# A gated recurrence with a gated convolution: one exponential for two chunks, products in place, other rings and a new order

## The chip, the core and the metric

The kernel runs on one core of a Trainium2 chip. The metric is the device time of one execution in microseconds (us). The core has five instruction queues that run side by side and meet only at semaphores: PE (matmuls and transposes; PEld is its weight load), DVE, ACT (activation functions by table), POOL and SP (which here only issues transfers). Each queue works strictly in the order in which its instructions were written.

## What is computed

Inputs are x, r_gate and i_gate, each 4 x 6336 x 256 in float32, and small weights. With c = 8:

```python
log_a = c * sig_r * np.log(a_base)          # a_base = sigmoid(a_param), clipped
a_t = np.exp(log_a)
norm = np.sqrt(np.maximum(1.0 - a_t * a_t, 1e-06))
x_gated = norm * sig_i * x
h = a_t[:, t] * h + x_gated[:, t]           # for each t in a sequence
```

Then the states h pass a causal convolution of 5 taps for each of the 256 channels; its sigmoid is the gate, and the output is (gate * (h @ w_val)) @ w_out, again 4 x 6336 x 256 in float32.

## The kernel before

The 25,344 rows of the four sequences are one line of time. It is cut into 50 windows of 512 rows (the last has 256), and the windows into 27 chunks: windows 0 and 1 are a chunk each, then come 23 chunks of two windows, then window 48 and window 49. Channels are handled as two halves of 128.

A window passes these steps. `lr`, `li`, `lx` load r, i and x (512 KB each; issued on SP, `load`). `th` makes the tanh of half of r and i in one ACT instruction of 2048 columns (L292); a sigmoid is half of that plus one. The gated input u is (tanh + 1) * x: either POOL does it in two instructions (`pp`, L300, and `up`, L312) or DVE in two of 512 columns (`uv`, L317). For a chunk, `tr` transposes the tanh of r on PE so that channels lie on the partitions (L326), and `ex` makes the decay a of it, one ACT exponential for each half, read from a PSUM bank and written to the ring `aring` (L333), with scale and bias taken for each partition from `khf`. `sq`, `sv` or `sa` square the decay on POOL (L344), DVE (L348) or ACT (L352) into `ering`. `rt` takes the square root of 1 - a*a for a batch of chunks (mostly three, six windows) on ACT (L363); it needs another function table, so each of the eleven batches has a table load ahead of it and one behind it (L495). `nt` transposes the norm back (L376), `xg` multiplies it with u on DVE (L383), `xt` transposes the product (L394), and `sc` runs the recurrence over a chunk and a half as one scan on DVE (L415), into `yring`. Where that ring starts again, a copy of its last four columns goes ahead (L411, on ACT, eight times). `cv` is the convolution as matmuls with diagonal weights (L427), `tg` its tanh (L434), `vl` the value product (L442), `gv` gate times value on DVE (L447), `ou` the output matmuls in two parts (L458), `cd` or `ca` copies each part out of PSUM on DVE or ACT (L466, L468), and `st` stores the window.

Every ring is a tile with a fixed number of slots: `riring` and `xring` four windows, `tring` three, `uring` ten, `xgring`, `tgring` and `gvring` two, `oring` four. A step that fills a slot waits until the step that last read it is done. PSUM has eight banks, and the words of the order name which a step uses.

The order of all instructions is one written list, `ORDER`; there is no planner at work when the kernel is built. A word such as `tr.8@6,7` is a step, its window or chunk, and its banks. The words of one engine, taken in the order of the list, are that engine's queue; `lr`, `li`, `lx` and `st` are SP's.

Of the kernel before, what the change touches and what calls it, by code (L numbers as in the profile page):

```python
# [8 lines left out]
P = 128  # L9
# [14 lines left out]
NU = 10  # L24
# [3 lines left out]
NXG = 2  # L28
NTG = 2
NGV = 2  # L30
NOSB = 4

ORDER = """
s_ident s_small s_kt s_diag li.0 lr.0 th.0 li.1 lr.1 th.1 pp.1 lr.2 li.2 tr.0@0,1 tr.1@2,3 ex.0.1 sq.0.1 ex.0.0 sq.0.0
s_wl.2 lx.2 li.3 lx.0 li.4 th.2 ex.1.0 sv.1.0 ex.1.1 rt.0 sv.1.1 rt.1 lx.1 uv.0 lr.3 nt.0@3 xg.0 lr.4 nt.1@2 xt.0@1,0
th.3 up.1 xg.1 xt.1@3,2 uv.2 th.4 li.5 pp.4 tr.2@4,5 lr.5 th.5 ex.2.1 ex.2.0 lx.3 tr.3@6,7 ex.3.0 sc.0.1 uv.3 lx.4
li.7 up.4 s_wl.0 lr.7 ex.3.1 th.7 lr.6 sa.3.1 li.6 th.6 tr.4@6,7 sq.2.0 lx.5 s_wl.3 sv.2.1 sv.3.0 rt.2 uv.5 sc.1.1
sc.0.0 cv.0@0,1 lx.6 sc.1.0 nt.2@3 s_wl.1 s_wcast pp.6 lx.7 lx.8 li.8 uv.7 li.10 li.9 lr.8 lr.9 ex.4.1 lr.10 li.11
nt.3@2 ex.4.0 nt.5@4 xg.2 xg.3 xt.2@3,2 th.8 sc.2.0 xg.5 tg.0 vl.0@6,7 gv.0 up.6 pp.8 th.9 tr.5@0,1 nt.4@3 xg.4 th.10
cv.1@4,5 sq.4.1 up.8 ex.5.1 lr.11 th.11 tr.6@3,1 ou.0.0@6 ou.0.1@7 lx.10 ex.5.0 tg.1 lx.9 ex.6.1 ex.6.0 uv.10 uv.9  # L40
sc.2.1 cd.0.0 li.13 li.12 lr.12 lr.13 xt.3@4,5 vl.1@0,1 cv.2@2,3 gv.1 sc.3.0 li.14 lr.14 sc.3.1 lx.14 lx.13 li.15
th.12 li.16 lx.12 th.13 lx.11 lr.17 lr.15 lr.16 tg.2 cv.3@0,1 tg.3 tr.7@6,4 ex.7.1 vl.2@2,3 ex.7.0 li.17 ou.1.0@0
pp.11 sq.5.0 sq.6.1 sq.6.0 sq.5.1 sq.4.0 pp.12 rt.3 cv.4@4,5 gv.2 tg.4 ou.2.0@6 cd.2.0 pp.13 ou.1.1@1 vl.3@2,3 gv.3
up.12 cd.1.1 cd.1.0 cd.0.1 st.1 up.11 sq.7.1 th.14 ou.3.1@2 ou.3.0@3 cd.3.0 cd.3.1 th.15 st.0 st.3 ou.2.1@1 cv.5@6,7
tg.5 cd.2.1 st.2 up.13 lx.17 nt.7@2 xg.7 nt.6@1 xg.6 pp.14 up.14 pp.15 vl.4@2,3 gv.4 nt.8@1 xt.4@4,5 xg.8 th.16 lx.16
pp.16 vl.5@2,3 li.18 lx.15 li.19 lr.19 nt.9@1 tr.8@6,7 ex.8.0 sc.4.0 sq.8.0 th.17 sc.4.1 lr.18 ou.4.1@0 cd.4.1
ou.4.0@4 lr.21 xg.9 lr.20 li.20 gv.5 cv.7@5,6 ex.8.1 tg.7 cd.4.0 st.4 xt.5@0,1 ou.5.0@2 sc.5.1 cd.5.0 sc.5.0 pp.17
up.16 sq.8.1 cv.6@3,4 sa.7.0 ou.5.1@7 tg.6 cd.5.1 tr.9@5,6 ex.9.0 nt.10@1 xg.10 up.15 vl.6@2,3 ex.9.1 nt.11@4 st.5
vl.7@5,6 xg.11 cv.9@0,1 xt.6@7,4 th.19 li.23 gv.7 th.18 ou.7.0@5 gv.6 cv.8@2,3 li.21 sc.6.0 cd.7.0 tg.9 up.17 th.20
lx.18 lx.21 lx.20 li.22 tg.8 vl.9@0,1 ou.6.1@6 sc.6.1 ou.7.1@7 gv.9 cd.7.1 tr.10@2,3 cd.6.1 sq.9.0 ou.6.0@5 cd.6.0  # L50
vl.8@0,1 ou.9.0@7 lx.19 lr.22 gv.8 li.24 lr.24 ou.9.1@4 cd.9.1 cv.11@5,6 cd.9.0 st.7 st.9 st.6 ou.8.0@0 cd.8.0 sq.9.1
rt.4 nt.13@4 xg.13 nt.12@7 xg.12 pp.19 pp.20 up.20 pp.18 up.18 up.19 tg.11 ex.10.1 sq.10.1 vl.11@0,1 gv.11 th.21 pp.21
lr.25 nt.14@4 xt.7@7,6 up.21 cv.10@0,1 tg.10 ex.10.0 sq.10.0 th.22 ou.8.1@5 tr.11@0,1 nt.15@3 sc.7.1 sc.7.0 xg.15
vl.10@6,7 ou.11.1@3 ex.11.1 sq.11.1 ex.11.0 xg.14 xt.8@2,4 lr.23 gv.10 ou.10.0@6 lx.23 th.23 pp.23 up.23 lx.22
# [52 lines left out]
def kernel(  # L107
# [34 lines left out]
    def places(cap, lens):  # L142
        at, out = 0, []
        for n in lens:
            if at + n > cap:
                at = 0
            out.append(at)
            at += n
        return out

    a_at = places(NA, clen)
    e_at = places(NE, clen)

    segs, y_at, y_wrap = [], [], []
    at = 4
    for c in range(NCH):
# [370 lines left out]
```

## Time and profile before

| what | us |
|---|---|
| runs | 307.43, 307.86, 308.36 (median 307.86) |
| profiled execution, its time | 307.03 |
| profiled execution, its span | 305.2 |
| busy: ACT, DVE, PE, POOL | 284.7, 262.3, 241.6, 222.4 |
| moved by the transfers | 104.75 MB, mean 343 GB/s |

The span runs from the first to the last instruction; some 1.8 us lie around it. "Busy" counts instructions that compute. A row of the groups reads: line, engine, operation, output and inputs with their shapes, how many; then busy time of the group, mean duration of one in ns, and the idle time of the engine just before them with what ended it. A wait reads: who waited, for whom, us in total, how often, the longest.

### The profile page before, as it was taken

How to read it: one execution, taken by the hardware profiler on the slowest of the kernel's cores; microseconds unless marked ns; L12 is line 12 of the kernel's file. 1: busy time of each engine (PE TensorE's matmuls, PEld its weight loads, DVE VectorE, ACT ScalarE, POOL GpSimd, SP SyncE). 2: the span in 40 equal slices, each digit the busy share in tenths (PEclk: the TensorE clock that was granted, in tenths of full speed). 3: DMA queues.
4: the chain of work that ended last, by engine and by line, in shares of the span. 5: the costliest groups of instructions: out<-in, count | busy, mean ns of one | idle time of the engine just before them, and what ended most of it. 6: DMA issues, size and time to landing. Idle time of an engine off the chain costs nothing.

```text
span 305.2 us, 6266 instructions
## 1 busy us (share of the span) xinstructions
PE 241.6 (79%) x2463; PEld 165.8 (54%) x2463; DVE 262.3 (86%) x257; ACT 284.7 (93%) x234; POOL 222.4 (73%) x144
## 2 busy tenths in 40 slices
PE   0252386879698888978897996698998999999994
PEld 0241253546565656556664665466565675676663
DVE  2068895978999999899999999789999999999982
ACT  6899989999999998999999998989999999989664
POOL 1326636997999699999997899979996876626000
PEclk9998577999999999999999999979999999999999
DMA  7999999999999999999999799999999849633345
GB/s 266 390 409 404 389 407 362 414 407 402 349 414 341 412 350 415 372 410 412 379 410 407 294 384 387 396 338 413 400 406 383 269 183 307 246 140 141 137 164 216
DMA packets 29419, 104.75 MB, mean 343 GB/s; under 512 B 3271, under 2 KB 3790, under 8 KB 29390
## 3 DMA queue, kind: packets, MB, share of 16 engines
q1 hardware_dynamic: 29376, 104.35, 88.7%
q8 instruction: 19, 0.31, 0.4%
q14 instruction: 10, 0.08, 0.1%
q10 hardware_dynamic: 14, 0.01, 0.0%
HBM read 78.39 MB, written 25.95 MB: 342 GB/s over the span
## 4 chain that ended last, share of the span: by engine, by line
DMA 25%; PE 22%; ACT 17%; POOL 16%; issue 10%; DVE 7%; SPq 2%; ACTq 0%; POOLq 0%; DVEq 0%
DMA xring<-in_x_dram 15%; POOL uring L312 9%; ACT tring L292 8%; PE banks L427 8%; PE banks L458 6%; DMA riring<-in_r_gate_dram 5%; PE banks L442 5%; POOL ering L344 5%; ACT aring L333 4%; DMA out_dram<-oring 4%; POOL tring L300 3%; ACT tgring L434 3%; DVE uring L317 2%; PE banks L376 2%; DVE gvring L447 2%
## 5 line engine op out<-in xcount | busy, mean ns | idle before, releaser
L415 DVE TENSOR_TENSOR_SCAN yring<-aring,yring,banks 128x1024 bf16<-128x1024 f32 (+5 forms) x52 | 104.7, 2035 | 1.3 <-PE banks L394 1.1
L312 POOL TENSOR_TENSOR uring<-tring,xring 128x1024 bf16<-128x1024 bf16 (+1 forms) x43 | 91.1, 2132 | 17.5 <-DMA xring<-in_x_dram 16.5
L292 ACT ACTIVATE tring<-riring 128x2048 bf16<-128x2048 f32 (+1 forms) x50 | 93.6, 1901 | 5.8 <-DMA riring<-in_r_gate_dram 2.4
L344 POOL TENSOR_TENSOR ering<-aring 128x1024 f32<-128x1024 f32 (+2 forms) x47 | 84.9, 1826 | 13.2 <-ACT aring L333 13.1
L427 PE MATMUL banks<-yring,diag 64*64 64x512 bf16 (+7 forms) x1060 | 66.3, 376 | 7.6 <-ACT aring L333 2.0
L447 DVE SCALAR_TENSOR_TENSOR gvring<-tgring,banks 128x1024 bf16<-128x1024 bf16 (+1 forms) x50 | 59.2, 1201 | 7.8 <-PE banks L442 2.8
L300 POOL TENSOR_SCALAR tring<-tring 128x1024 bf16<-128x1024 bf16 (+1 forms) x43 | 44.3, 1039 | 24.7 <-ACT tring L292 24.6
L333 ACT ACTIVATE aring<-banks,khf 128x1024 f32<-128x1024 bf16 (+2 forms) x54 | 59.6, 1142 | 1.3 <-PE banks L326 1.2
L458 PE MATMUL banks<-wo,gvring 128*128 128x256 bf16 x396 | 54.9, 274 | 4.2 <-DVE gvring L447 2.9
L442 PE MATMUL banks<-yring,wv 128*128 128x512 bf16 (+4 forms) x212 | 50.2, 364 | 5.0 <-ACT tgring L434 2.5
L434 ACT ACTIVATE tgring<-banks 128x1024 bf16<-128x1024 f32 (+1 forms) x50 | 50.3, 1025 | 2.2 <-PE banks L427 1.7
L458 PEld LDWEIGHTS <-gvring 128*128 128x128 bf16 x396 | 41.6, 114 | 17.0 <-issue 7.2
L326 PE MATMUL banks<-ident_b,tring 128*128 128x128 bf16 x396 | 31.0, 232 | 24.9 <-ACT tring L292 19.1
L427 PEld LDWEIGHTS <-diag 64*64 64x64 bf16 x1060 | 31.3, 108 | 31.8 <-issue 17.8
L466 DVE COPY oring<-banks 128x512 f32<-128x512 f32 x68 | 44.1, 678 | 4.1 <-DMA out_dram<-oring 2.3
L363 ACT ACTIVATE ering<-ering 128x4096 bf16<-128x4096 f32 (+4 forms) x14 | 44.7, 3219 | 0.1
L376 PE MATMUL banks<-ident,ering 128*128 128x128 f32 x198 | 35.0, 307 | 10.7 <-ACT ering L363 8.0
L326 PEld LDWEIGHTS <-tring 128*128 128x128 bf16 x396 | 25.9, 104 | 31.6 <-ACT tring L292 23.3
L383 DVE TENSOR_TENSOR xgring<-banks,uring 128x1024 bf16<-128x1024 bf16 (+1 forms) x50 | 32.9, 675 | 9.2 <-POOL uring L312 4.2
L376 PEld LDWEIGHTS banks<-ident,ering 128*128 128x128 f32 x198 | 29.2, 207 | 18.6 <-ACT ering L363 10.3
L442 PEld LDWEIGHTS <-wv 128*128 128x128 bf16 x212 | 19.7, 98 | 23.3 <-issue 10.2
L394 PE MATMUL banks<-ident,xgring 128*128 128x128 f32 x198 | 27.8, 279 | 3.1 <-DVE xgring L383 2.0
(35 smaller groups left out, 110.6 us busy)
## 6 DMA issues: line engine op xcount, KB each, us to landing
riring<-in_i_gate_dram SPq DMA_DIRECT2D x49, 512.0 KB, 7.5
riring<-in_r_gate_dram SPq DMA_DIRECT2D x49, 512.0 KB, 7.8
xring<-in_x_dram SPq DMA_DIRECT2D x49, 512.0 KB, 7.9
out_dram<-oring SPq DMA_DIRECT2D x49, 512.0 KB, 6.3
oring<-in_moe_w_val_dram SPq DMA_DIRECT2D x1, 256.0 KB, 5.9
riring<-in_r_gate_dram SPq DMA_DIRECT2D x1, 256.0 KB, 6.3
riring<-in_i_gate_dram SPq DMA_DIRECT2D x1, 256.0 KB, 6.3
xring<-in_x_dram SPq DMA_DIRECT2D x1, 256.0 KB, 3.6
```

The costliest lines, as they stand in the source:

```text
L292: nc.scalar.activation(out=tring[:, w % NTRI, :, 0:J, :], in_=riring[:, w % NRI, :, 0:J, :], func=ACT.Tanh, scale=0.5)
L312: nc.gpsimd.tensor_tensor(out=u, in0=t1, in1=xt, op=ALU.mult)
L326: nc.tensor.transpose(out=bank[:, o:o + P], in_=tring[:, w % NTRI, 0, j, h * P:(h + 1) * P], identity=ident_b[:])
L333: nc.scalar.activation(out=aring[:, h, a_at[c]:a_at[c] + clen[c]].rearrange("c (w p j) -> c w p j", w=nw, p=P), in_=bank[:, 0:clen[c]].rea ...
L344: nc.gpsimd.tensor_tensor(out=e, in0=a, in1=a, op=ALU.mult)
L376: nc.tensor.transpose(out=bank[:, (q * H + h) * P:(q * H + h + 1) * P], in_=ering[:, o + h * clen[c] // 2 + q:o + h * clen[c] // 2 + wins[ ...
L415: nc.vector.tensor_tensor_scan(out=yring[:, h, col:col + o1 - o0], data0=aring[:, h, a_at[c] + o0:a_at[c] + o1], data1=xT[:, o0:o1], initi ...
L427: nc.tensor.matmul(out=gp[oh * 64:oh * 64 + 64, h, a:b], lhsT=diag[half * 64:half * 64 + 64, h, k, :], rhs=yring[half * 64:half * 64 + 64, ...
L434: nc.scalar.activation(out=tgring[:, w % NTG, :, 0:wins[w]], in_=live.pop(("gp", w))[:, :, 0:wins[w]], func=ACT.Tanh, scale=0.5)
L442: nc.tensor.matmul(out=val[:, m, a:b], lhsT=wv[:, hk, m * P:(m + 1) * P], rhs=yring[:, hk, col:col + b - a], start=(hk == 0), stop=(hk == ...
L447: nc.vector.scalar_tensor_tensor(out=gvring[:, w % NGV, :, 0:wins[w]], in0=tgring[:, w % NTG, :, 0:wins[w]], scalar=1.0, in1=live.pop(("va ...
L458: nc.tensor.matmul(out=ops[:, e * D:(e + 1) * D], lhsT=gv[:, hk, j:wins[w]:J], rhs=wo[:, hk, :], start=(hk == 0), stop=(hk == H - 1))
```

## The change

Groups of chunks are introduced. From chunk 2 to chunk 23 two neighbouring chunks form a group. The transposes of the tanh of r are now written for a group and one half at a time (`tr.c.h`), 16 of them into two neighbouring banks, and one exponential of 2048 columns reads both banks. Chunks 0, 1, 24, 25 and 26 stay alone. So 54 exponentials become 32.

To keep the tanh of r of four windows until then, a slot of `tring` gets three parts in place of two: i has the middle one, and r lies ahead of it or behind it, changing with each turn of the ring (`swapped`). The load puts r and i into `riring` in the matching order.

The product with the norm is written over u (`xgring` goes, `uring` gets 11 slots), and the gated value over the gate (`gvring` goes, `tgring` gets 3 slots). The 64-column identity of the set-up lies in an output slot. The eight copies at the wrap of `yring` move from ACT to DVE.

The list `ORDER` is another one throughout. By count, `ca` goes from 31 to 37 and `cd` from 68 to 62; `uv` from 7 to 10 windows, `pp` and `up` from 43 to 40; `sq` from 47 to 46, `sv` from 4 to 5, `sa` stays 3. Windows with `uv` were 0, 2, 3, 5, 7, 9, 10 and are 0, 2 to 7, 10, 12, 13. All other steps are as many as they were, and the same batches of square roots are taken.

```diff
-NU = 10
+NU = 11
-NXG = 2
-NTG = 2
-NGV = 2
+NTG = 3
+GROUPS = [[0], [1], [2, 3], [4, 5], [6, 7], [8, 9], [10, 11], [12, 13], [14, 15], [16, 17], [18, 19], [20, 21], [22, 23],
+    [24], [25], [26]]
...
-        tring = rings.tile([P, NTRI, 2, 4, D], BF16, name="tring")
-        xgring = rings.tile([P, NXG, 2, D, 2], BF16, name="xgring")
+        tring = rings.tile([P, NTRI, 3, 4, D], BF16, name="tring")
-        gvring = rings.tile([P, NGV, H, 512], BF16, name="gvring")
+        id64 = oring[:, 0, 0, 0:64]
...
+        def swapped(w):
+
+            return (w // NTRI) % 2
+
...
-                dst = riring[:, w % NRI, "ri".index(which), 0:J, :]
+                dst = riring[:, w % NRI, "ri".index(which) ^ swapped(w), 0:J, :]
...
-            nc.scalar.activation(out=tring[:, w % NTRI, :, 0:J, :], in_=riring[:, w % NRI, :, 0:J, :],
+            a = swapped(w)
+            nc.scalar.activation(out=tring[:, w % NTRI, a:a + 2, 0:J, :], in_=riring[:, w % NRI, :, 0:J, :],
...
+        def op_tr(c, h, *at):
+            ws = [w for k in sorted(group_of[c], key=lambda k: a_at[k]) for w in cwins[k]]
+            J = wins[ws[0]] // P
+            bank = banks[:, at[0]:at[-1] + 1].rearrange("c k n -> c (k n)").bitcast(BF16)
+            for g, w in enumerate(ws):
+                assert wins[w] == J * P
+                for j in range(J):
+                    o = (j * len(ws) + g) * P
+                    nc.tensor.transpose(out=bank[:, o:o + P],
+                                        in_=tring[:, w % NTRI, 2 * swapped(w), j, h * P:(h + 1) * P],
+                                        identity=ident_b[:])
+            live["rT", c, h] = bank
...
+            at = sorted(a_at[k] for k in group_of[c])
+            n = clen[c]
+            J = wins[cwins[c][0]] // P
+            src = bank[:, 0:n * len(at)].rearrange("c (j k q) -> c k q j", j=J, k=len(at))
...
+            nc.scalar.activation(out=dst, in_=src, func=ACT.Exp, scale=khf[:, h:h + 1], bias=khf[:, h:h + 1])
...
-            nc.vector.tensor_tensor(out=xgring[:, w % NXG, 0:nq].rearrange("p q d two -> p (q d two)"),
+            nc.vector.tensor_tensor(out=uring[:, w % NU, 0:nq].rearrange("p q d two -> p (q d two)"),
...
-                        nc.scalar.copy(out=yring[:, :, 0:4], in_=yring[:, :, e - 4:e])
+                        nc.vector.tensor_copy(out=yring[:, :, 0:4], in_=yring[:, :, e - 4:e])
...
-            nc.vector.scalar_tensor_tensor(out=gvring[:, w % NGV, :, 0:wins[w]],
+            nc.vector.scalar_tensor_tensor(out=tgring[:, w % NTG, :, 0:wins[w]],
```

## The prediction

> **What bounds the kernel now.** I read the busy shares first, then the groups with their shapes kept apart, then what ScalarE waited for, and last the stretches between the square-root batches (`rt.0` to `rt.10`). The busy shares:
>
> ```profile
> PE 241.6 (79%) x2463; PEld 165.8 (54%) x2463; DVE 262.3 (86%) x257; ACT 284.7 (93%) x234; POOL 222.4 (73%) x144
> ```
>
> ACT has 20.5 us free in the whole span, and DVE 42.9. The stretches below are cut where ACT loads the table for a batch of square roots (65.3, 97.0, 131.5, 156.7, 189.9, 225.4, 252.6 and 278.6 us, `rt.3` to `rt.10`); the columns are the start and end, the length, then busy time of PE, PEld, DVE, ACT and POOL, the granted clock, the DMA share and GB/s.
>
> ```profile
> 20.00:40.00 20.00, 8.09 (x78) 5.62 (x77) 16.08 (x15) 19.89 (x14) 12.85 (x10) 0.70 1.03 399
> 40.00:66.00 26.00, 19.91 (x189) 13.50 (x190) 20.79 (x18) 25.13 (x20) 18.08 (x12) 0.90 1.01 395
> 66.00:98.00 32.00, 27.12 (x267) 18.50 (x265) 29.83 (x29) 31.94 (x24) 30.05 (x19) 1.00 1.01 381
> ...
> 225.00:252.60 27.60, 25.85 (x289) 18.35 (x288) 27.00 (x27) 27.52 (x26) 21.38 (x14) 1.00 0.79 292
> 252.60:278.50 25.90, 25.04 (x256) 16.95 (x254) 25.05 (x21) 24.42 (x28) 14.24 (x12) 1.00 0.61 223
> 278.50:305.20 26.70, 22.44 (x232) 14.24 (x229) 19.32 (x18) 17.21 (x25) 2.53 (x2) 0.99 0.42 168
> ```
>
> There are two regimes. From 20 to 252.6 us ACT is full in every stretch (27.52 of 27.60). After 252.6 us it is PE: 25.04 of 25.90, then 22.44 of 26.70, of which the last 4 us are the final copy and store. The DMA share stands at about 1.0 up to 225 us, so the transfers are a close second, but ACT hardly waits for them:
>
> ```profile
> ACT oring L468 <- PE banks L458: 4.7, 7, 2.3
> ACT tring L292 <- DMA riring<-in_r_gate_dram: 2.4, 2, 1.5
> ACT tgring L434 <- PE banks L427: 1.7, 2, 1.2
> ...
> ACT tring L292 <- POOL ering L344: 1.2, 1, 1.2
> ...
> ACT tring L292 <- POOL uring L312: 0.7, 3, 0.3
> ```
>
> The rows that price the change (busy us of the group, mean ns of one):
>
> ```profile
> L292 ACT ACTIVATE tring<-riring 128x2048 bf16<-128x2048 f32 x49 | 92.6, 1918 | 5.6 <-DMA riring<-in_r_gate_dram 2.4 <-POOL ering L344 1.2 <-issue 0.8
> L333 ACT ACTIVATE aring<-banks,khf 128x1024 f32<-128x1024 bf16 x46 | 54.0, 1215 | 0.0
> ...
> L468 ACT COPY oring<-banks 128x512 f32<-128x512 f32 x31 | 17.5, 598 | 4.7 <-PE banks L458 4.7
> ...
> L333 ACT ACTIVATE aring<-banks,khf 128x512 f32<-128x512 bf16 x6 | 4.4, 774 | 1.2 <-PE banks L326 1.2
> ```
>
> **The change, ACT.** Twenty-two pairs of exponentials of 1024 columns become 22 of 2048 (11 groups, two halves). The exponential rows give (1215 - 774)/512 = 0.861 ns a column, so 2048 columns cost 1215 + 882 = 2097 ns, against 2 x 1215 = 2430: 333 ns saved. Neighbours overlap by 1215 - 54.0/46 = 41 ns, and one overlap goes with each merge: 292 ns, times 22 = 6.4 us off. No 2048-column exponential stands in the trace. At worst it costs the two it replaces (0 saved). At best it costs what the 2048-column tanh does, 1918 (22 x 471 ns = 10.4 saved). I keep 6.4, from the same instruction's own rows. Its source now steps over two PSUM banks, 1024 bytes between neighbours instead of 256; the slope above already holds for a stepped read, so I add nothing.
>
> ACT takes six output copies from DVE (37 against 31): 6 x 17.5/31 = +3.4. The eight tiny copies at the wrap of the y ring leave it (8 x 201 ns, -1.6). It squares three full chunks instead of two and a 256-column one (1069 - 437 ns, +0.6). Table loads stay at 22. Sum -4.0: ACT would be busy 280.7.
>
> What counts is where this falls. Ahead of `rt.9` (its table load at 252.57) stand all merges but also 15 output copies instead of 6 (+5.1), six of the tiny copies (-1.2) and the extra square (+1.1): -6.4 + 5.1 - 1.2 + 1.1 = **-1.4 us on the path**. The rest of the ACT relief lies behind 252.6 us, beside a full PE, and is worth nothing there.
>
> **DVE.** Minus six output copies (6 x 44.1/68 = -3.9). Ten windows instead of seven have their gated input made here: 6 more instructions of 512 columns, mean 11.9/14 = 0.85, +5.1 (717 ns at the least, 2449 at the most: +4.3 to +14.7). One more square of 1024 columns, +2.8 (twice the 692 ns of the 512 form to 2.91: +1.4 to +2.9). The eight wrap copies, nearest the 168 ns copy of 10 columns, +1.3 (from 62 ns, a memset: 0.5 to 1.6). Sum +5.3, DVE 267.6. About 7.9 of it lies before the batch at 65 us; later DVE gets lighter. Its cover is ACT's full queue; the rival below is that cover failing.
>
> **POOL.** Three windows leave: 3 x (1049 + 2155) = -9.6. Two full squares fewer and one more of 256 columns, -3.3. Sum -12.9, POOL 209.5. ACT waited 1.2 + 0.7 for POOL; I take half of that away, **-1.0**.
>
> **PE.** The same transposes and matmuls. By the written order the work behind `rt.9` is 42.0 us before and 41.9 after (counts of the steps, at 1.21 for a window's convolution, 0.86 for its value product, 0.44 for a half of its output, 0.47 and 0.43 for the two transposes, all from single pieces of the chain of waits), so the PE-bound end of 52.6 us stays: **0**. Each half's transposes now fill two banks and are read for 2.1 us instead of 1.2, so these banks come free later; other banks are named for the steps in between, and ACT's order keeps another ACT instruction between the last tanh of a group and its exponential in all groups but the first (chunks 2 and 3), where it waits for 4 transposes, 4 x 0.064 = 0.3.
>
> **Rings and products in place.** The product with the norm goes into the ring of gated inputs and the gated value into the ring of the gate. An in-place DVE instruction stands beside one that is not, on 2 columns (169 ns each), so the instruction costs 0; between a gain and a loss I see no row that excludes a few ns. What changes is when a slot is free: the gate's slot now waits for the output matmuls of three windows earlier, where it had waited for the product of two windows earlier; measured in ACT work of the written order these waits have a mean lead of 4.7 us against 5.8, and some leads of nothing in both. The r half of a tanh slot is kept for six windows instead of three, which is what a group of four windows needs. The identity of 64 columns moves into an output slot that the first output needs only after 57 us: 0.
>
> **SP.** The same 204 transfers in a new order. The first four loads are the same four, so the first tanh instructions do not move. Leads of loads ahead of their tanh, in ACT work, are 15.2 against 15.6 us on average, two landing times of 7.5; 0, with 1 us either way for a few that come close.
>
> **The sum.** -1.4 - 1.0 + 0 + 0 = -2.4. The profiled execution took 307.03 for its span of 305.2, so 304.6; the median of the runs shown, 307.86, lies 0.8 above that execution, and by it the change gives 305.4. I say 305.0.
>
> **The rivals.**
> DVE starts the kernel late. Up to 66 us DVE has 51 us from its first square at 14.95, is busy for 40.1 of them and idle for 11. The moved work of 7.9 fits if the idle time can be filled. But the tanh of a window overwrites the slot whose gated input of three windows before must have been read, and in the new order windows 2 to 7 have it read by DVE, so a late DVE stops ACT. If none of the idle can be used, 7.9 - 2.4 = +5.5; if the moved instructions all run at their dearest (14.7 + 2.9 = 17.6), 6.6 overrun the 11 and 6.6 - 2.4 = +4.2. Time 309 to 312.5. It decides from 2.4 us of lateness on. For it: of the idle time between 15 and 66 us, 4.2 are waits for POOL's products and 2.4 for loads of x, which DVE cannot fill at will. Against it: with three products fewer on POOL just there, the first of these should shrink.
> The Trainium skill, "SBUF — State Buffer", section "Who interferes with whom", has a rule that speaks for this rival: a VectorE instruction with two SBUF inputs contends with a GpSimd one that reads SBUF, and the later waits for the other's whole length. The trace agrees: while DVE's two full squares ran (27.02 to 32.63) a POOL square took 2.88 us against its mean of 1.93. By that rule alone all six would be dear, and the overrun of 6.6 the case to expect.
>
> The transfers bind. At 370 to 404 GB/s and a share of about 1.0 from 40 to 225 us, the loads may not come faster; then ACT's relief turns into waits for loads: 307.0 to 307.9. Against it: the stretch from 131 to 158 us ran at 404.
>
> The plan fits better everywhere: ACT's whole -4.0 and the 1.9 of POOL waits come off: 301.1 to 302.
>
> The merge does not pay: two banks read at the price of two exponentials, -2.4 + 6.4 = +4.0: 311.
>
> **How the numbers follow.** A measurement of this kernel can tell 0.3%, about 0.9 us, from no change. Forecast 0.42 (303 to 306.5), better plan 0.15, transfers 0.11, late DVE 0.28, no merge 0.04. Faster 0.57, same 0.11, slower 0.32. The range of 8 in 10 goes down to the forecast with the merge at its best price (4.0 more saved, 300.6), which takes in the better plan, and up to 312, all of the late DVE but its far end: 300.5 to 312.
>
> **What would show it.** The exponential row at 128x2048, x22, near 2.10 us; ACT busy near 281; the table load of `rt.9` near 250.2; PE full from there, for some 52 us. Against me: idle time of ACT's tanh put down to DVE before 70 us, instructions of the gated input on DVE near 2.4 us, or PE idle behind 252 us waiting for gates.

## The result and the profile after

The changed kernel takes 311.57 us (median of four runs, 310.63 to 312.62); the kernel before took 307.88 (307.43 to 308.36) beside it. The ratio is 1.012, with a 95% interval from 1.0084 to 1.0157: 3.7 us slower, where 2.9 us faster was forecast; the time lies within the forecast's range, on the other side of no change. The profiled execution of after took 311.38 us for a span of 309.6; before it was 307.03 for 305.2. Medians are of all executions; the ratios leave out those more than 1.5% above the fastest of their kernel, of which run a4 below had four in thirteen (312 to 320 us, its profiled one among them) and no other run more than one.

The busy shares of after:

```profile
PE 238.7 (77%) x2439; PEld 166.0 (54%) x2463; DVE 267.6 (86%) x266; ACT 283.1 (91%) x210; POOL 209.9 (68%) x137
```

ACT works 1.6 us less, DVE 5.3 more, POOL 12.5 less, in a span that is 4.4 us longer. So what was lost is idle time: ACT has 26.5 us of it, where it had 20.5. The groups of after by shape, first on ACT (the joined exponential, the output copies), then on DVE (gated input, wrap copy, squares); columns as before: busy us of the group, mean ns of one, idle time ahead of them:

```profile
L346 ACT ACTIVATE aring<-banks,khf 128x2048 f32<-128x2048 bf16 x22 | 44.7, 2060 | 2.1 <-DVE yring L425 1.1 <-PE banks L330 0.7
...
L478 ACT COPY oring<-banks 128x512 f32<-128x512 f32 x37 | 20.2, 595 | 3.2 <-DMA out_dram<-oring 2.0 <-PE banks L468 1.2
```

```profile
L319 DVE SCALAR_TENSOR_TENSOR uring<-tring,xring 128x512 bf16<-128x512 bf16 x20 | 15.4, 831 | 9.8 <-DMA xring<-in_x_dram 9.5 <-ACT tring L294 0.3
L421 DVE COPY yring<-yring 128x8 bf16<-128x8 bf16 x8 | 6.8, 854 | 0.0
L358 DVE TENSOR_TENSOR ering<-aring 128x1024 f32<-128x1024 f32 x3 | 5.3, 1758 | 0.0
```

All exponentials together went from 59.6 to 52.6 us, as the merge was meant to. One row stands out: a copy of 8 columns that takes 854 ns. The 9.5 us that the gated input on DVE waits for loads of x (2.4 before) came over from POOL with the work: POOL's own wait for x fell from 16.5 to 8.4 us, so that the two together wait 17.9 us where they waited 18.9. The stretches of after, the last three cut at the table loads of `rt.9` and `rt.10` (255.6 and 287.3 us):

```profile
20.00:40.00 20.00, 7.25 (x60) 5.72 (x64) 15.72 (x20) 18.17 (x10) 5.42 (x3) 0.81 1.03 399
40.00:66.00 26.00, 17.92 (x175) 12.28 (x169) 16.73 (x15) 23.52 (x16) 16.34 (x12) 0.82 1.02 403
66.00:98.00 32.00, 23.57 (x219) 15.73 (x220) 30.67 (x31) 31.50 (x21) 25.10 (x15) 1.00 0.96 364
...
225.00:255.60 30.60, 28.75 (x319) 20.40 (x321) 30.60 (x32) 29.76 (x24) 22.16 (x14) 1.00 0.69 265
255.60:287.30 31.70, 29.45 (x310) 20.32 (x312) 31.50 (x24) 27.45 (x31) 16.37 (x13) 1.00 0.64 242
287.30:309.60 22.30, 16.70 (x167) 10.72 (x166) 15.54 (x19) 12.31 (x16) 0.00 (x0) 0.98 0.39 154
```

Read them against the rows of before. From 20 to 66 us every engine now does less: ACT 41.69 against 45.02, DVE 32.45 against 36.87, POOL 21.76 against 30.93, PE 25.17 against 28.00, at the same DMA share. The work that is missing there comes later: from 225 to 287.3 us DVE is busy 62.1 of 62.3 us. The table loads say where the time is lost. `rt.3` starts at 73.57 us (65.34 before), `rt.4` at 96.99 (97.00), `rt.7` at 196.76 (189.87), `rt.8` at 224.17 (225.35), `rt.9` at 255.62 (252.57), and from `rt.9` to the end it takes 54.0 us in place of 52.6. The lateness of `rt.3` and `rt.7` is made good by the next batch. The loss that stays comes to light between `rt.8` and `rt.9` (31.45 us where 27.22 stood), and 1.4 us more behind `rt.9`. That is where it shows, not where it arose: DVE has 31.40 us of work between the two, where it had 26.77.

What ACT waited for in after, and two waits that grew, POOL's for the decays and PE's for exponentials (after, then before):

```profile
ACT tgring L444 <- PE banks L437: 6.5, 6, 2.2
ACT tring L294 <- DMA riring<-in_r_gate_dram: 3.5, 5, 0.8
ACT oring L478 <- DMA out_dram<-oring: 2.0, 1, 2.0
...
ACT tring L294 <- POOL uring L314: 1.1, 1, 1.1
```

```profile
POOL ering L354 <- ACT aring L346: 30.3, 13, 10.8
PE banks L437 <- ACT aring L346: 6.8, 3, 3.9
```

```profile
POOL ering L344 <- ACT aring L333: 13.1, 5, 4.0
PE banks L427 <- ACT aring L333: 2.0, 5, 0.6
```

ACT waits 4.8 us more for the convolutions on PE (6.5 against 1.7). The convolutions in turn wait 4.8 us more for exponentials that still read their banks (6.8 against 2.0); all of the 6.8 lies before 104 us, the longest one (3.92) from 50.0 to 53.9 us, until the first joined exponential of chunks 4 and 5 has read banks 0 and 1.

POOL's squares wait 17.2 us more for the exponentials, but only a part of that is a chunk waiting for its neighbour. Of the 30.3 us, 9.5 stand before 20 us, nearly all at chunk 0, which stays alone (in before POOL waited 9.6 there for a tanh). One wait of 10.8 is at the first group, yet its squares begin at 27.75 us, where before began chunk 2's at 28.67: POOL has fewer products ahead of them. Another 5.8 lie between 66 and 225 us, where all chunks are joined and before had none of this wait, and 4.2 behind 225 us, where before had all of its 13.1. Around the early group [6, 7] the trace of after shows such a wait (ACT, POOL, ACT):

```profile
63.60 4.00 ACT L346 ACTIVATE aring<-banks,khf 128x2048 f32<-128x2048 bf16 x2
```

```profile
67.68 1.89 POOL L354 TENSOR_TENSOR ering<-aring 128x1024 f32<-128x1024 f32 x1 [2.21 <-ACT aring L346]
```

```profile
69.29 1.93 ACT L444 ACTIVATE tgring<-banks 128x1024 bf16<-128x1024 f32 x2
71.65 1.91 ACT L294 ACTIVATE tring<-riring 128x2048 bf16<-128x2048 f32 x1 [0.42 <-DVE uring L319]
73.57 1.28 ACT L505 ACT_TABLE_LOAD   x1
```

`rt.3` takes chunks 4, 5 and 6; chunk 6 is joined with 7, so its decays begin at 63.6 us, where they began at 55.4 before. But this wait is not what ACT stands at: the last square of the batch ends at 69.57, and ACT then does the two gate tanhs and the tanh that the list puts ahead of `rt.3`. In all the new list has 17 tanhs ahead of `rt.3` where the old one had 14, at 1.9 us each, so most of its 8.2 us of lateness is written into the order.

### The profile page after: what moved, and what is told of

It is laid out like the page before. It is cut to its first block, busy times and chain, and to the rows that moved or that the text cites. A ratio compares the mean times of both kernels' runs of the same rounds, so it can differ in the third digit from the quotient of the medians.

```text
span 309.6 us, 6220 instructions
## 1 busy us (share of the span) xinstructions
PE 238.7 (77%) x2439; PEld 166.0 (54%) x2463; DVE 267.6 (86%) x266; ACT 283.1 (91%) x210; POOL 209.9 (68%) x137
## 4 chain that ended last, share of the span: by engine, by line
DMA 30%; DVE 22%; PE 21%; ACT 15%; issue 8%; SPq 1%; POOL 1%; ACTq 0%; DVEq 0%; POOLq 0%
DMA riring<-in_i_gate_dram 13%; DVE yring L425 11%; DMA riring<-in_r_gate_dram 10%; PE banks L437 6%; PE banks L452 5%; DMA out_dram<-oring 5%; PE banks L468 4%; DVE tgring L457 4%; ACT aring L346 4%; ACT ering L373 4%; DVE oring L476 4%; ACT tring L294 3%; DMA xring<-in_x_dram 3%; PE banks L404 2%; PE banks L386 2%
## 5 line engine op out<-in xcount | busy, mean ns | idle before, releaser
L354 POOL TENSOR_TENSOR ering<-aring 128x1024 f32<-128x1024 f32 (+2 forms) x46 | 80.9, 1776 | 30.3 <-ACT aring L346 30.3
L314 POOL TENSOR_TENSOR uring<-tring,xring 128x1024 bf16<-128x1024 bf16 (+1 forms) x40 | 85.1, 2138 | 14.7 <-DMA xring<-in_x_dram 8.4
L457 DVE SCALAR_TENSOR_TENSOR tgring<-tgring,banks 128x1024 bf16<-128x1024 bf16 (+1 forms) x50 | 59.1, 1200 | 5.6 <-ACT tgring L444 2.9
L468 PE MATMUL banks<-wo,tgring 128*128 128x256 bf16 x396 | 53.3, 274 | 10.7 <-DVE tgring L457 5.8
L346 ACT ACTIVATE aring<-banks,khf 128x2048 f32<-128x2048 bf16 (+3 forms) x32 | 52.6, 1673 | 2.9 <-PE banks L330 1.5
L468 PEld LDWEIGHTS <-tgring 128*128 128x128 bf16 x396 | 41.3, 115 | 23.1 <-issue 11.1
L452 PE MATMUL banks<-yring,wv 128*128 128x512 bf16 (+7 forms) x188 | 47.7, 366 | 4.9 <-ACT tgring L444 2.0
L476 DVE COPY oring<-banks 128x512 f32<-128x512 f32 x62 | 39.8, 678 | 2.2 <-PE banks L330 2.0
L393 DVE TENSOR_TENSOR uring<-banks,uring 128x1024 bf16<-128x1024 bf16 (+1 forms) x50 | 32.6, 675 | 5.3 <-PE banks L386 5.2
L404 PE MATMUL banks<-ident,uring 128*128 128x128 f32 x198 | 28.4, 287 | 2.9 <-DVE uring L393 2.6
```

What stands on the lines that cost most here:

```text
L314: nc.gpsimd.tensor_tensor(out=u, in0=t1, in1=xt, op=ALU.mult)
L346: nc.scalar.activation(out=dst, in_=src, func=ACT.Exp, scale=khf[:, h:h + 1], bias=khf[:, h:h + 1])
L354: nc.gpsimd.tensor_tensor(out=e, in0=a, in1=a, op=ALU.mult)
L452: nc.tensor.matmul(out=val[:, m, a:b], lhsT=wv[:, hk, m * P:(m + 1) * P], rhs=yring[:, hk, col:col + b - a], start=(hk == 0), stop=(hk == ...
L457: nc.vector.scalar_tensor_tensor(out=tgring[:, w % NTG, :, 0:wins[w]], in0=tgring[:, w % NTG, :, 0:wins[w]], scalar=1.0, in1=live.pop(("va ...
L468: nc.tensor.matmul(out=ops[:, e * D:(e + 1) * D], lhsT=gv[:, hk, j:wins[w]:J], rhs=wo[:, hk, :], start=(hk == 0), stop=(hk == H - 1))
```

## The experiments

Every run was timed beside the kernel before on the same chip. To compare runs of different chips I use the ratios, and a difference between two kernels in us is the difference of their ratios times 307.9. With intervals of about 1 us to either side for each, such a difference is known to 1.5 or 2 us. In the expectations of the first eight runs "theory A" is that VectorE's load is what the new kernel lost by; in the later ones that theory is called V, and A stands for ScalarE setting the pace.

**Four parts of the change, one at a time**

a1: the kernel after, with the wrap copies on ACT again.

```diff
-                        nc.vector.tensor_copy(out=yring[:, :, 0:4], in_=yring[:, :, e - 4:e])
+                        nc.scalar.copy(out=yring[:, :, 0:4], in_=yring[:, :, e - 4:e])
```

> The changed kernel with one part undone: the eight wrap copies of the y ring are on ACT again. Theory A (DVE paces the changed kernel from about 190 us on, and the copies on DVE are held by POOL: 6.8 us busy for eight, of which 3.3 us lie at 241 and 268 us where DVE has no idle time): the time falls by 3 to 6 us, from 311.6 to 305.5 to 308.5. Theory B (the new order loses its time before 75 us, in DVE waiting for loads of x and in ACT waiting for loads of r): the copies come after 86 us and are beside the point, less than 1.5 us off. Theory C (the wider exponentials are to blame, by holding banks): no more than 1 us off.

Measured: 309.74 us, ratio 1.007 (1.0039 to 1.0101), so 1.5 us less than after. DVE's busy time falls by 4.7 to 262.9, and ACT does the eight copies in 1.5 us. This is the one part of the change whose undoing gave time back, and the gain is just as large as its error. Why the copies are dear is seen in after, DVE first, then POOL:

```profile
86.63 0.80 DVE L421 COPY yring<-yring 128x8 bf16<-128x8 bf16 x1
87.35 2.33 DVE L425 TENSOR_TENSOR_SCAN yring<-aring,yring,banks 128x1024 bf16<-128x1024 f32 x1
```

```profile
84.51 1.04 POOL L302 TENSOR_SCALAR tring<-tring 128x1024 bf16<-128x1024 bf16 x1 [4.33 <-ACT tring L294]
85.52 3.74 POOL L354 TENSOR_TENSOR ering<-aring 128x1024 f32<-128x1024 f32 x2
```

The copy ends at 87.43. POOL's two squares, one behind the other, take 1.87 each, so the first ends at 87.4. Six of the eight copies end within 0.05 us of the end of POOL's instruction under way; the other two, with POOL at rest, take 0.14 and 0.16. The Trainium skill, "SBUF — State Buffer", section "Who interferes with whom", says that a copy in one of VectorE's two-port modes contends with GpSimd and that the one that comes second is blocked for the whole of the other's instruction; the trace agrees for these six, with 0.45 to 1.75 us against 0.14. That a copy of 8 columns runs in such a mode is shown by no run here.

a2: the kernel after, each exponential of 2048 columns issued as two of 1024 in the same place, from the same banks.

```diff
+            if len(at) == 2:
+                for k in range(2):
+                    nc.scalar.activation(out=aring[:, h, at[k]:at[k] + n].rearrange("c (q j) -> c q j", j=J),
+                                         in_=src[:, k], func=ACT.Exp, scale=khf[:, h:h + 1], bias=khf[:, h:h + 1])
+                return
```

> The changed kernel with each 2048-column exponential issued as two of 1024 columns, in the same place, from the same two banks; nothing else moves. ACT gets 7 us more work (22 x 0.33). Theory A (DVE paces): ACT has 26 us idle and takes it up, at most 2 us longer, 311.6 to 313.6. If ACT still paces the stretch from 20 to 250 us, as the prediction had it, 4 to 7 us longer: 315.5 to 318.5. Theory C (the width itself hurts): equal or faster.

Measured: 312.43 us, ratio 1.0159 (1.0109 to 1.021): 1.2 us more than after, at ACT 288.1 busy, 5.0 more. So the merge, taken by itself, saves 5 us of ACT's time and about 1 us of the kernel's; no saving at all lies within the error.

a3: the kernel after, windows 4, 6, 12 and 13 with their gated input made on POOL again.

```diff
-uv.3 th.6 li.8 lr.8 uv.4 xg.0 th.7 uv.5
+uv.3 th.6 li.8 lr.8 pp.4 up.4 xg.0 th.7 uv.5
...
-lx.13 uv.13 ex.6.0
+lx.13 pp.13 up.13 ex.6.0
```

> The changed kernel with the gated input of windows 4, 6, 12 and 13 made on POOL in two instructions instead of on DVE, words replaced where they stand. DVE loses 8 instructions, 6 to 7 us, all before 72 us; POOL gets 8 more, 12.8 us, where it was idle most of the time (28 of the first 66 us busy). Theory A with DVE late from the start: 2 to 4 us faster, 307.5 to 309.5. Theory B with the loads of x as the cause: the loads do not come sooner, POOL's products wait for them in DVE's place, DVE is freed: 1 to 3 us faster. If POOL's squares come late behind the waiting products, slower by 1 to 4.

Measured: 311.64 us, ratio 1.0127 (1.0086 to 1.0168), as after. DVE is 2.9 us lighter and nothing comes of it. These products lie ahead of 72 us, and up to 66 us DVE has 27.1 us of idle time.

a4: the kernel before, with only the wrap copies moved to DVE.

```diff
-                        nc.scalar.copy(out=yring[:, :, 0:4], in_=yring[:, :, e - 4:e])
+                        nc.vector.tensor_copy(out=yring[:, :, 0:4], in_=yring[:, :, e - 4:e])
```

> The kernel before with one part of the change alone: the eight wrap copies on DVE. If the copy is held until the POOL instruction under way ends, each costs 0.15 to 2.1 us on DVE, some 6 us in all. Theory A: DVE paced the kernel before in part as well (92% busy from 98 us on), so 1 to 4 us slower, 309 to 312. If DVE's idle time there takes it up: within 1 us of 307.9.

Measured: 308.3 us, ratio 0.9991 (0.9953 to 1.0028): by the ratio the copies cost nothing in the old order. Against the 1.5 us of the new order that is a difference of 1.8 us with an error of 1.9, so whether the order changes their price is not shown. The profile is of an execution of 318.74 us, so only one copy is read from it, with POOL below it:

```profile
L411 DVE COPY yring<-yring x1: 12418/12418/12418, 141.0 to 141.0; 128x8 bf16<-128x8 bf16 x1
```

```profile
139.77 3.74 POOL L344 TENSOR_TENSOR ering<-aring 128x1024 f32<-128x1024 f32 x2
143.49 2.04 POOL L300 TENSOR_SCALAR tring<-tring 128x1024 bf16<-128x1024 bf16 x2
145.51 2.14 POOL L312 TENSOR_TENSOR uring<-tring,xring 128x1024 bf16<-128x1024 bf16 x1
147.61 3.73 POOL L344 TENSOR_TENSOR ering<-aring 128x1024 f32<-128x1024 f32 x2
151.31 2.12 POOL L312 TENSOR_TENSOR uring<-tring,xring 128x1024 bf16<-128x1024 bf16 x1
```

The copy of 8 columns began at 141.0, under the first of these eight POOL instructions, and ended at 153.4 with the last of them, when POOL came to rest. It was not let in between them, as the six copies of after were; the block by one instruction alone does not describe it.

**The rings and the groups in the old order**

b1: the old order, with the new rings: `tring` in three parts, the product with the norm written over u (10 slots in `uring`), the identity in an output slot. No group. The gate's product in place was left out.

```diff
-        tring = rings.tile([P, NTRI, 2, 4, D], BF16, name="tring")
-        xgring = rings.tile([P, NXG, 2, D, 2], BF16, name="xgring")
+        tring = rings.tile([P, NTRI, 3, 4, D], BF16, name="tring")
...
-tr.8@6,7
+tr.8.0@6 tr.8.1@7
```

> The kernel before with some of the ring changes alone: three parts in a slot of the tanh ring with r changing sides, the product with the norm written over the gated input (10 slots), the small identity in an output slot, transposes written a half at a time. Order, exponentials of 1024 columns, the gate's own ring and the wrap copy on ACT stay as before. If rings and products in place cost anything by themselves, it shows here. Expected by all theories: the time of the kernel before within 0.5%, 306.5 to 309.7.

Measured: 307.28 us, ratio 0.9969 (0.9938 to 1.0): the rings cost nothing and may give 1 us. It is also the fastest kernel of this study that does the whole computation, though its lead over the kernel before is no larger than its error.

b2: b1 with nine groups joined, each at the place of its later chunk, and the rest of the list as it was. b3: b2 with each exponential of 2048 issued as two of 1024, as in a2.

```diff
+GROUPS = [..., [2, 3], [4, 5], [6, 7], [8, 9], [10, 11], [12, 13], [14, 15], [16], [17], [18], [19], [20, 21], [22, 23], ...]
```

> The old order and those rings with the merge alone: nine groups (chunks 2 to 15 and 20 to 23) take one exponential of 2048 columns a half, at the place of the later chunk; transposes and squares of the earlier chunk move behind the later one's, all else stands. ACT saves 18 x 0.3 = 5.4 us in an order where it has hardly a free moment to 250 us. If the merge as such pays and the new order lost it (theory D): 303.5 to 306.5, faster than the kernel before. If a group of four windows holds up decays, squares and square roots by as much as it saves (theory E): 307 to 311.

> The same order as the run before, but each 2048-column exponential issued as two of 1024 columns in the same place: the late decays of the earlier chunk without the saving. Theory D (the lateness is covered): 307.5 to 309.5. Theory E (lateness is what costs): 310 to 314. The difference to the run before is what the merge saves on ACT in the old order: 4 to 5.4 us if ACT paces, 1.2 as in the new order if it does not.

Measured: b2 361.52 us (ratio 1.1705, 1.1637 to 1.1772), b3 361.16 (1.1712). Joining the exponentials without a new order costs 53 us, and the number of instructions has no part in it. The largest wait of b2 is POOL's:

```profile
POOL ering L359 <- ACT aring L351: 78.6, 12, 12.6
```

Squares stand in POOL's queue in order; one whose decays wait for the next chunk's windows holds up every product behind it, and with those the tanh of later windows (ACT's waits for these products go from 0.7 to 11.4 us). It is not the only wait that grew: ACT waits 19.5 us for convolutions, where it waited 1.7. Between `rt.6` and `rt.7`, whose chunks 16 to 19 stayed alone, b2 needs 33.2 us and before 33.1: nothing is lost where nothing is joined.

d4: b1 with one group, chunks 14 and 15.

```diff
+GROUPS = [..., [13], [14, 15], [16], ...]
...
-tr.14.0@1 tr.14.1@0 up.27 ex.14.0 ex.14.1 sq.14.0 sq.14.1
...
-tr.15.0@6 tr.15.1@2 ex.15.1 cd.17.1
+tr.14.1@2,3 tr.14.0@4,5 ex.14.1 ex.14.0 sq.14.0 sq.14.1 cd.17.1
```

> The old order in the new rings (307.3 us) with one pair joined, chunks 14 and 15, whose decays are made in two exponentials of 2048 where the later chunk's stood. Where nine pairs cost 53 us, batch 5 to batch 6, which holds this pair alone, lost 10 us. Theory L (each chunk that waits for its neighbour holds up squares, square roots, norms and gates in their queues): +5 to +10, so 312 to 317. Rival (only several pairs together cost that; one is taken up by later slack): 306.5 to 309.

Measured: 312.85 us, ratio 1.0167 (1.0111 to 1.0224): 6.1 us more than b1, from one pair. Its trace shows two long waits, POOL's for the joined decays and ACT's for a convolution, and `rt.6` 7.5 us later than in b1 (156.20); the last line is PE's:

```profile
154.21 3.74 POOL L361 TENSOR_TENSOR ering<-aring 128x1024 f32<-128x1024 f32 x2 [6.13 <-ACT aring L353]
```

```profile
159.34 1.02 ACT L451 ACTIVATE tgring<-banks 128x1024 bf16<-128x1024 f32 x1 [5.20 <-PE banks L444]
...
163.68 1.28 ACT L512 ACT_TABLE_LOAD   x1
```

```profile
154.18 1.97 PE L411 MATMUL banks<-ident,uring 128*128 128x128 f32 x8 [3.21 <-ACT aring L353]
```

The second wait does not come from the first. In PE's queue the transposes `xt.11@5,4` stand ahead of that convolution, and they wait 3.21 us for bank 4 or 5, which the second joined exponential reads until 154.1: the edit gave the pair banks 2 to 5. Both ways end together ahead of `rt.6`, POOL's squares at 163.76 and ACT's queue at 163.68. So one pair costs some 6 us where the list makes room neither for its late decays nor for its second bank, and this run does not tell the two apart; nor do b2 and b3, which have the same words there. The new order, with eleven groups, ends 3.7 us behind.

**Taking the wait out of the new order: three runs that failed to**

d1: the kernel after with all groups taken apart, the first chunk's transposes and exponentials moved ahead to the tanh of its own last window. d2: group [6, 7] alone taken apart, the squares of chunks 4 to 6 and `rt.3` moved ahead. d3: d2 with the wrap copies on ACT.

```diff
-th.11 xg.4 s_wcast tr.4.1@6,7 tr.4.0@0,1 ex.4.0 up.9 ex.4.1
+th.11 tr.6.1@3 tr.6.0@2 xg.4 s_wcast tr.4.1@6,7 tr.4.0@0,1 ex.4.0 ex.6.1 ex.6.0 up.9 ex.4.1 sq.4.0 sq.5.1 sq.4.1 sq.6.1
...
-ex.6.0 tr.6.1@6,7 ex.6.1 li.16 lr.16 th.16
+ex.7.0 tr.7.1@6 ex.7.1 rt.3 li.16 lr.16 th.16
```

> The kernel after with all eleven groups taken apart: the first chunk's transposes and exponentials stand right behind the tanh of its own last window, the second chunk's where the group's stood; the other words are in their old order. Against the run that only split the exponentials in place (312.4 us) this has the same instructions, but decays of every other chunk some 2 to 8 us earlier. Theory L (waiting for the second chunk's windows costs time in the new order): 308 to 310.5. Rival P (the order was planned around the groups; squares, square roots and norms stand where they stood in their queues, and nobody asks for the early decays): 311.5 to 313.5.

> The kernel after with group [6, 7] alone taken apart, chunk 6's decays and the squares of chunks 4 to 6 ahead, and the square root of batch 3 (rt.3) moved six tanhs earlier in ScalarE's list, to right behind chunk 7's decays: about 69 us in place of 73.6. Theory L (the lag of the output side that is set up there stays to the end): 308.5 to 310.5. Rival P (VectorE is full later on and the lag is taken up by then): 311 to 312.5.

> The run before this one with the eight wrap copies on ScalarE as well (alone, they gave 1.9 us). Theory L: 306.5 to 309. Rival P: 309.3 to 310.5, the copies' own gain and nothing more.

Measured: d1 371.38 us (ratio 1.2044, 1.1979 to 1.2108), d2 329.88 (1.07, 1.0651 to 1.075), d3 326.31 (1.0596, 1.055 to 1.0642). No theory had this. The trace of d2, ACT:

```profile
50.08 1.91 ACT L294 ACTIVATE tring<-riring 128x2048 bf16<-128x2048 f32 x1 [1.11 <-DMA riring<-in_i_gate_dram]
56.96 6.20 ACT L346 ACTIVATE aring<-banks,khf 128x2048 f32<-128x2048 bf16 x4 [4.97 <-PE banks L330]
...
76.22 1.28 ACT L505 ACT_TABLE_LOAD   x1
```

The moved transposes of chunk 6 need the tanh of window 11, which starts at 50.08 us, and the 32 transposes of group [4, 5], which in after PE had done by 50.02, now stand behind them in its queue: PE does all 48 up to 56.9, ACT waits 4.97 us for it, and `rt.3`, written earlier, starts later (76.22 against 73.57). These runs do not answer what the waiting of the first chunk costs in the new order. They show that a place in a list is a place in five queues, and that a list made for one set of instructions does not bear moving a few of them by hand.

b4 fell the same way: a1 with four output copies of the end on ACT instead of DVE.

```diff
-cd.36.1 sc.21.0 sq.24.1 sq.23.1 lr.48 cd.36.0 st.36 sc.21.1 rt.9
+ca.36.1 sc.21.0 sq.24.1 sq.23.1 lr.48 ca.36.0 st.36 sc.21.1 rt.9
```

> The changed kernel with the wrap copies on ACT and four of DVE's late output copies (both of window 36, the first of 43 and of 44) given to ACT as well, words replaced where they stand: 2.7 us off DVE between 240 and 290 us, where it is busy for 62.2 of 63 us and ACT has 3.5 us idle. Theory A (DVE paces the end): 1.5 to 2.7 us faster than with the wrap copies on ACT alone, 307 to 308.5. If it is PE or the length of the chain that ends the kernel: no change, 309.7.

Measured: 316.71 us, ratio 1.028 (1.023 to 1.033), 6.5 us more than a1. Copies that ACT has in its queue ahead of `rt.9` wait for the output matmuls there (ACT's waits for these go from 1.2 to 3.9 us), and the batch comes 3.5 us later than in a1 (257.53 against 254.04); the rest is lost behind it.

**What work is worth, added and taken away**

c1 and c3: ten output copies of windows 25 to 31 on DVE issued twice, in after and in before. c2 and c4: four tanhs (windows 39 to 42) on ACT issued twice.

```diff
-                nc.vector.tensor_copy(out=dst, in_=src)
+                for _ in range(1 + ((w, i) in TWICE)):
+                    nc.vector.tensor_copy(out=dst, in_=src)
```

> The kernel after, with ten of VectorE's output copies (cd of windows 25 to 31, of about 0.68 us each, between 224 and 252 us) issued twice: 6.8 us more for VectorE alone, at a time when it is busy 62.8 of 63 us. Theory V (VectorE sets the pace of the kernel after from 224 us on): +5 to +7 us over after (311.6), so 316.5 to 318.5. Theory A (ScalarE still sets the pace): at most +2, so 311.5 to 313.5.

> The kernel after, with four of ScalarE's tanhs (th of windows 39 to 42, 1.92 us each) issued twice: 7.7 us more for ScalarE alone. Theory V: ScalarE's idle time (26.5 us in all) takes most of it in, +0 to +3 us over after (311.6). Theory A: +6 to +8, so 317.5 to 319.5.

> The kernel before, with ten of VectorE's output copies (cd of windows 25 to 30) issued twice: 6.8 us more for VectorE alone. Theory A, on which the prediction rested (ScalarE alone paces the kernel before): at most +2 over before (308), so 308 to 310. Rival B (in the kernel before too VectorE and ScalarE pace it together, so that relief of one alone is worth little): +4 to +7, so 312 to 315.

> The kernel before, with four of ScalarE's tanhs (th of windows 39 to 42) issued twice: 7.7 us more for ScalarE alone. Theory A and rival B both: +5 to +8 over before, so 313 to 316; under +3 would say that ScalarE does not pace the kernel before either, at that place, and that its 7 us of relief were worth little from the start.

e1: after without the ten copies of c1, whose rows of the output are then not made. e2: before, with 18 exponentials of the even chunks cut from 1024 to 672 columns, so that the decays left out are those of an earlier chunk.

```diff
+            q = 84 if c in SHORT else P
...
-                in_=bank[:, 0:clen[c]].rearrange("c (w j p) -> c w p j", w=nw, p=P), func=ACT.Exp,
+                in_=bank[:, 0:clen[c]].rearrange("c (w j p) -> c w p j", w=nw, p=P)[:, :, 0:q], func=ACT.Exp,
```

> The kernel after without the ten output copies that the run with more VectorE work issued twice (the second or both halves of windows 25 to 31 are left out, so those rows of the output are not the result): 6.8 us less for VectorE late, no word moved. Theory V (VectorE's fuller queue is what the kernel after lost by): -4 to -6.5 against after (311.6), so 305 to 307.5. Rival C (VectorE, ScalarE and TensorE hand the work to and fro in fixed orders; what one is relieved of is waited for by the others): 309.5 to 311.5.

> The kernel before with the exponentials of the nine even chunks from 6 to 22 cut from 1024 to 672 elements a row (352 elements at 0.83 ns, so 0.29 us each, 18 times: 5.3 us less for ScalarE; the decays left out are those of an earlier chunk, so the output is not the result): ScalarE's saving by the joined exponentials, without their wait, their order or anything on VectorE. The prediction's step (ScalarE paces, so its relief is on the path): -4 to -6 against before (308), so 302 to 304. Rival C: -0 to -2, so 306 to 308.

| run | what | ratio (95%) | us against its own kernel | worth of 1 us (error) |
|---|---|---|---|---|
| c1 | after, DVE +6.8 | 1.0333 (1.0298 to 1.0368) | +6.6 | 0.97 (0.2) |
| c2 | after, ACT +7.7 | 1.0418 (1.0376 to 1.046) | +9.2 | 1.19 (0.2) |
| c3 | before, DVE +6.8 | 1.0154 (1.0111 to 1.0196) | +4.7 | 0.70 (0.2) |
| c4 | before, ACT +7.7 | 1.0251 (1.0209 to 1.0293) | +7.7 | 1.00 (0.2) |
| e1 | after, DVE -6.8 | 1.0092 (1.0064 to 1.0121) | -0.9 | 0.13 (0.2) |
| e2 | before, ACT -5.3 | 0.9951 (0.9924 to 0.9978) | -1.5 | 0.28 (0.2) |

The two halves of this table do not mirror each other. Work added late goes to the end at seven tenths or more, on either engine and in either kernel; work taken away comes back at about a quarter or less. Only c1 and e1 are at the same place: c4 adds to ACT late, and e2 relieves it from chunk 6 to chunk 22, so that late relief of ACT is not tried. And in its profile e1 relieves DVE by 3.0 us only (264.6 busy): the output copies fall by 6.4, but the wrap copies take 8.4 us instead of 6.8 and the gated input 16.5 instead of 15.4. Where ACT's time went in e2 is seen in its waits, and in its exponentials, which did become 0.30 us shorter:

```profile
L336 ACT ACTIVATE aring<-banks,khf 128x1024 f32<-128x1024 bf16 x28 | 32.7, 1212 | 0.0
L336 ACT ACTIVATE aring<-banks,khf 128x672 f32<-128x672 bf16 x18 | 15.8, 908 | 0.0
```

```profile
ACT tring L294 <- POOL uring L314: 4.0, 6, 1.4
ACT tgring L437 <- PE banks L430: 2.9, 4, 1.2
...
ACT tring L294 <- POOL ering L347: 2.1, 1, 2.1
```

The profiled execution of e2 took 308.37 us (span 306.6), 1.8 more than its median, so it shows where ACT's time went and not the gain. In it ACT is busy 280.2 us, 4.5 less than before; it waits 4.2 more for POOL (4.0 + 2.1 against 0.7 + 1.2) and 1.2 more for PE (2.9 against 1.7). `rt.6` starts 1.5 us earlier than in before (155.26), `rt.7` at the same time (189.80), `rt.8` 1.6 later (226.92). POOL could not be faster: from 132 to 158 us it is busy 26.00 of 26.00 us in before and in e2. The transfers could hardly be either: their share is 1.02 there, and by 225 us before has moved 86.4 MB and e2 85.9 (lengths times GB/s of six stretches each). In e1 DVE is 2.3 us lighter from 225 to 255.6 us, and the table loads of `rt.9` and `rt.10` stand at 256.07 and 287.76, where after had 255.62 and 287.31.

## Why the prediction was wrong

**The joined exponential.** Right: 2060 ns where 2097 were worked out, 7.0 us off the group where 6.4 were. ACT's busy time was not: 283.1 for 280.7. By the groups the parts add up to -5.3 (exponentials -7.0, output copies +2.7, wrap copies -1.6, squares +0.6), yet busy time fell by 1.6. Neighbours on ACT overlap by about 0.1 us (a copy of 0.19 us begins at 144.70 in d4 and its successor at 144.79), and there are 24 instructions fewer to overlap: 2.4 us by that estimate, where the sum took 41 ns for each merge; 1.3 stays unplaced.

**"-1.4 us on the path", the first step that failed.** It rested on the reading that ACT is full from 20 to 252.6 us and so sets the pace, and that time taken off it comes back whole. ACT is busy for 94% or more of every stretch there; but beside it, from 66 to 225 us, POOL is busy about nine tenths or more and the transfers' share is 0.96 to 1.02, and from there DVE and PE are nearly full (26.77 and 25.45 of 27.20 us between `rt.8` and `rt.9` of before). The chain of work that ended last, followed back through the profile of before, lies on ACT for 17% of the span only (before, then after):

```profile
DMA 25%; PE 22%; ACT 17%; POOL 16%; issue 10%; DVE 7%; SPq 2%; ACTq 0%; POOLq 0%; DVEq 0%
```

```profile
DMA 30%; DVE 22%; PE 21%; ACT 15%; issue 8%; SPq 1%; POOL 1%; ACTq 0%; DVEq 0%; POOLq 0%
```

e2 makes such a saving, with nothing else changed: 1 us of ACT is worth 0.28 of the kernel. The Trainium skill, "Perfetto Trace Analysis", section "Identifying the Most-Contended Engine", says to take the engine with the highest occupancy, or for the transfers the use of memory bandwidth, and to optimize that first. Among the engines that is ACT, and e2 does not agree that it pays; no run here relieves the transfers. `rt.9` came at 255.62 where 250.2 was named.

**DVE's +5.3, covered by ACT's full queue: cost 0.** The sum came out exactly (267.6) by errors that cancel: the wrap copies +6.8 for 1.3 (row: 168 ns for a copy that reads PSUM; measured 854 for one that reads SBUF), the squares +0.3 for 2.8 (1758 ns for 2842), the gated input +3.5 for 5.1, output copies -4.3 for -3.9; these four make +6.3, and the other rows and overlaps take 1.0 off. The cover was not there late in the kernel: c3 prices DVE's added time at 0.70 in the kernel before, and c1 at 0.97 in after, where DVE's share of the chain went from 7% to 22%. Early it was: a3 takes 2.9 us off DVE and gains nothing. And "later DVE gets lighter" was read from the count of steps ahead of a batch; by the clock DVE does 38.9 us of work up to 66 us instead of 42.0, and 8.3 more behind it.

**POOL -12.9.** Right in size (209.9 for 209.5). The gain of 1.0 on ACT's waits for POOL was at most 0.5 (1.1 + 0.3 left of 1.9). What was not priced at all is the other direction: that the first chunk of a group gets its decays late. In after POOL waits 5.8 us for joined decays between 66 and 225 us, where it waited for none. b2, b3 and d4 show what joining costs where the list makes no room for it, there together with the second bank.

**PE's end.** 54.0 us for 52.6. The same steps stand behind `rt.9`; PE is busy 46.2 of them by its records instead of 47.5 (24 of its 2463 matmuls are missing in this trace), so it is waiting that was added. That the two banks of a half come free later was named in the forecast and put at nothing because the steps in between have other banks; up to 104 us PE's convolutions wait 6.8 us for them in after, against 2.0 in all of before. What that costs the kernel was not tried: a2 splits the exponential but reads the same banks.

**Rings, in place, SP: 0.** b1 agrees for the rings and the product with the norm (-1.0, interval up to 0). The gate's product and SP's order were not tried alone.

**The rivals.** The late DVE gave the right time (309 to 312.5) by the wrong place: ACT's tanh waited 0.4 us for DVE before 75 us, and the gated input ran at 831 ns in the mean and 1.84 us at the most, not at 2.4. That the transfers bind was set at 0.11; their share and e2 speak for it as one of three limits, but as it was put, relief turning into waits for loads, it makes the kernel no faster and not slower. That the merge does not pay (+4.0) has its time near the result, but its reason is refuted by the row of 2060 ns.

**What adds up.** The forecast named 305.0 and 311.6 came. Rings -1.0, merge -1.2, wrap copies +1.5, as measured one by one, make -0.7, so that 4.4 us are left to the new order with all that it moves; the error of that remainder is some 2.5 us, and it holds if the parts simply add. So two steps failed. Of the 2.4 us of relief for ACT, put on the path whole, 0.7 would come back at the worth that e2 measured. And the new order's own waits, put at nothing under PE, rings and SP, are the larger term. Which of them it is stays open: the late decays, the banks held longer, or another place in the order. The late decays were argued from POOL's waits and from the old order, not shown in the new one: d1 to d3 broke the order before they could tell. a3 and e1 speak against DVE's added work as the whole of it.

## What to carry to other kernels

Before a saving on the busiest engine is put into a sum, look for how many others are above 90% in the same stretch: with three or four of them, as here, an added microsecond cost 0.7 to 1.2 and a saved one gave back a quarter or less. That relieving the others as well would help was not tried. Shortening the instructions in place, with nothing moved, tells by one run what such a saving is worth. And joining two instructions makes the first wait for the second's inputs and holds two buffers until both are read; these prices stand in no row of the trace before, and together they were 6 us for one pair in the old order.

## What the hardware showed that was not expected

A DVE copy of 8 columns within SBUF, 0.14 us with POOL at rest, ended with POOL's instruction under way (854 ns in the mean, 1.75 us at most in after) and once only after eight POOL instructions, at 12.42 us. DVE's square of 1024 columns took 1758 ns in the mean in after and 2842 in before. The three of after, in DVE's timeline:

```profile
30.22 2.88 DVE L358 TENSOR_TENSOR ering<-aring 128x1024 f32<-128x1024 f32 x1
35.35 1.20 DVE L358 TENSOR_TENSOR ering<-aring 128x1024 f32<-128x1024 f32 x1
66.59 1.20 DVE L358 TENSOR_TENSOR ering<-aring 128x1024 f32<-128x1024 f32 x1
```

The dear one began while POOL was squaring (27.75 to 32.01), the other two with POOL at rest, and both of before ran beside POOL (27.02 to 32.63). So the same instruction took 1.20 us alone and 2.88 beside POOL, and the 2.8 that the forecast took for one more square was the dear price.
